# Loading q and k as four tokens of 1 KB on two partition halves, with the last product in two column halves

## The chip, the cores and the metric

The kernel runs on one core of a Trainium2 chip. The metric is the device time of one execution in microseconds, as the median over repeated runs. Before the change the median of 11 runs is 303.47 us (303.08 to 305.29). A core has five engines that run beside each other: PE (TensorE, matrix products; its weight loads are listed apart as PEld), DVE (VectorE), ACT (ScalarE), POOL (GpSimd) and SP (SyncE, which issues most of the transfers here). Sixteen DMA engines move data between HBM and the on-chip memory SBUF, which has 128 partitions. Matrix products land in PSUM.

## What is computed

Attention inside chunks of 64 tokens, and then a bilinear feed-forward layer on its output:

```python
# q, k, v: [8 batches, 8 heads, 576 tokens, 64], float32; chunks of 64 tokens
scores = scale * np.matmul(q_c, k_c.transpose(0, 1, 2, 4, 3))
attn = np.exp(scores - max) / (sum + 1e-09)
x = np.matmul(attn, v_c)          # heads joined: [4608 tokens, 512]
a, b = x @ w_a, x @ w_b           # w_a, w_b: [512, 1536]
out = (a * b) @ w_out             # w_out: [1536, 512], out float32
```

## The kernel before

**Units and blocks.** The 4608 tokens are cut into 18 units of 256 tokens for the attention and into 9 blocks of 512 tokens (two units each) for the feed-forward part. The order of all work on all five engines is written out by hand: each engine runs its instructions in program order and waits where a value isn't there yet.

**Loading a unit.** `load` (line 187) issues the transfers of a unit's q, k and v on SP's queue, and `load_ab` (108) and `load_wo` (137) those of the weights. All of them write into one pool of eight staging tiles named `st`, 4 KB on each of 128 partitions, 512 KB each. A staging tile is free again when a cast (`cast`, 205; `cast_ab`, 117; `cast_wo`, 150) has turned it into 16-bit data. The casts run on POOL, except those of unit 0's q and k, which run on DVE. Since SP issues in order, a load that waits for a free tile holds back all loads behind it. Unit 5's k and all later units are transposed by DMA; q of units 0 to 5 and k of units 0 to 4 (`PE_UNITS`, line 11) are transposed by TensorE, and only those have the layout that the change touches. In this layout a partition holds two neighbouring tokens of all eight heads, so that one contiguous run in HBM is two tokens of one head: 512 bytes. A batch has 576 tokens, so a unit that crosses a batch border comes in two pieces (`pieces`, 168): unit 2 as 64 and 192 tokens, which are 32 and 96 partitions, and unit 4 as 128 and 128 tokens, which are 64 and 64 partitions. Units 0, 1, 3 and 5 are one piece over 128 partitions. v is loaded one token to a partition, in runs of 256 bytes; the panels of w_a and w_b have runs of 1 KB over 128 partitions.

**Transposing.** `transpose_pe` (218) makes eight 128x128 transposes of a tile, and two copies of 512 columns each (line 240) bring the result from PSUM into the tile `qkt`, in the order that `scores` (260) reads. `sums` (290), `inverse` (311) and `values` (318) finish the attention of a unit; the last step of `values` is two multiplies on DVE (line 337), which write the unit's part of `xT`.

**The start.** Lines 663 to 670 put the loads in this order: q and k of unit 0, q and k of unit 1, v of unit 0, panel wb 0, v of unit 1, panel wa 0, then the panels 1 and 2 and (line 682) 3. Then follow q and k of unit 2, panels 4 and 5, v of unit 2, unit 3, w_out, and units 4 and 5 (698 to 718). TensorE runs filler products (`keep_warm`, 97) between the first steps. From line 726 on it runs block 0 through `ab_step` (377), whose products stand at line 389: twelve steps, two for each weight panel, with the transposes of unit 2 behind steps 6 and 7. Block 1 follows with the transposes of units 3 (774, 776), 4 (789) and 5 (793) between its steps. Blocks 2 to 8 run in `Group` (421), with products at line 439.

**The end.** The last block's output is made in two `OutGroup` objects (525), one for each 128-row group `th`, in seven products (line 575) of six matmuls with 256 columns each. The last of them is number 6, first for `th` = 0 and then for `th` = 1. After it DVE scales 256 columns out of PSUM (line 608) and `store` (521) sends 128 rows x 256 columns to HBM, for `th` = 0 on SP's queue and for `th` = 1 on ACT's.

Of the kernel before, what the change touches and what calls it, by code (L numbers as in the profile page):

```python
# [10 lines left out]
PE_UNITS = {"q": 6, "k": 5, "v": 0}  # L11
AB_SCALE = 256.0
OUT_SCALE = 1.0 / AB_SCALE
# [3 lines left out]
def kernel(  # L17
# [10 lines left out]
    nc = tc.nc  # L28
    BF16 = mybir.dt.bfloat16
    FP32 = mybir.dt.float32  # L30
# [7 lines left out]
    B, H, S, D = q.shape  # L38
# [148 lines left out]
    def load(U, names="qkv"):  # L187

        for n in names if U < NU else "":
            src = {"q": q, "k": k, "v": v}[n]  # L190
            if U < PE_UNITS[n]:
                st = st_pool.tile([128, H, 2, D], FP32, name="st")
                for r, b, s, m in pieces(U):
                    nc.sync.dma_start(  # L194
                        out=st[r // 2:(r + m) // 2].rearrange("p h i d -> p h (i d)"),
                        in_=src[b, :, s:s + m, :].rearrange("h (p i) d -> p h (i d)", i=2),
                    )
                staged[n, U] = st.rearrange("p h i d -> p i h d")
            else:
                staged[n, U] = st_pool.tile([128, 2, H, D], FP32, name="st")  # L200
                load_natural(staged[n, U], src, U)
# [3 lines left out]
    def cast(U, names="qkv"):  # L205
        for n in names if U < NU else "":
            if U >= 4 and wo_sums:
                combine_wo(*wo_sums.pop(0))
            raw[n, U] = raw_pool.tile(
                [128, 2, H, D], BF16, name=f"{n}_raw"  # L210
            )
            eng = nc.vector if U == 0 and n != "v" else nc.gpsimd
            eng.tensor_copy(out=raw[n, U], in_=staged.pop((n, U)))


    qkt = {}

    def transpose_pe(U, names="qk"):
        if U not in qkt:
            qkt[U] = qkt_pool.tile([128, 2, 2, NKT, 128], BF16, name="qkt")  # L220
        for n in names:
            w = "qk".index(n)
            src = raw.pop((n, U))
            t = [bank() for _ in range(2 if U < 2 else 1)]
            tp = [
                t[i % len(t)].bitcast(BF16).rearrange("c (i m p) -> c i m p", i=2, m=NKT)[:, i]
                for i in range(2)
            ]
            for i in range(2):
                for m in range(NKT):  # L230
                    nc.tensor.transpose(
                        tp[i][:, m, :],
                        src[:, i, 2 * m:2 * m + 2, :].rearrange("p j d -> p (j d)"),
                        identity,
                    )
            dst = qkt[U][:, w].rearrange("c g m (p i) -> c i m g p", i=2)
            for i in range(2):
                on_dve = i == 0 if U == 0 else w == 0 or U == 1
                cp = nc.vector.tensor_copy if on_dve else nc.scalar.copy
                cp(out=dst[:, i], in_=tp[i].rearrange("c m (g p) -> c m g p", g=2))  # L240

    def transpose_dma(U):
        if U not in qkt:
            qkt[U] = qkt_pool.tile([128, 2, 2, NKT, 128], BF16, name="qkt")
        for w, n in ((0, "q"), (1, "k")):
            if U < PE_UNITS[n]:
                continue
            nc.sync.dma_start_transpose(
                out=qkt[U][:, w].rearrange("p g m c -> p (g m) c"),
                in_=raw.pop((n, U)).rearrange("p g h d -> p (g h d)"),  # L250
            )

# [5 lines left out]
    late = []  # L258

    def scores(U, pools=(None, None), now=2):  # L260
        t = qkt.pop(U)
        E_of[U] = sm_pool.tile([128, 2, NKT, 2, 64], BF16, name="E")
        sc = [bank(p).rearrange("p (m g s) -> p m g s", m=NKT, g=2) for p in pools]
        for m in range(NKT):
            for g in range(2):
                for j in range(2):
                    for cl in range(2):
                        nc.tensor.matmul(
                            sc[j][cl * 64:cl * 64 + 64, m, g, :],
                            t[j * 64:j * 64 + 64, 1, g, m, cl * 64:cl * 64 + 64],  # L270
                            t[j * 64:j * 64 + 64, 0, g, m, cl * 64:cl * 64 + 64],
                            start=m == 0 and g == 0,
                            stop=True,
                            skip_group_check=True,
                        )
        E = E_of[U]
        for j in range(2):
            late.append(
                lambda j=j: nc.scalar.activation(
                    out=E[:, j], in_=sc[j], func=AF.Exp, scale=scale  # L280
                )
            )
        exps(now)
# [34 lines left out]
    def values(U):  # L318
        E, rs, vr = E_of.pop(U), rs_of.pop(U), raw.pop(("v", U))
        K, u = divmod(U, 2)  # L320
        if u == 0:
            x_tiles[K] = x_pool.tile([128, NKT, BLK], FP16, name="xT")
        av = [bank().rearrange("p (m g s) -> p m g s", m=NKT, g=2) for _ in range(2)]
        for m in range(NKT):
            for g in range(2):
                for cl in range(2):
                    for j in range(2):
                        nc.tensor.matmul(  # L328
                            av[cl][j * 64:j * 64 + 64, m, g, :],
                            vr[cl * 64:cl * 64 + 64, g, 2 * m + j, :],  # L330
                            E[cl * 64:cl * 64 + 64, j, m, g, :],
                            start=True,
                            stop=True,
                        )
        for cl in range(2):
            x = x_tiles[K][:, :, 256 * u:256 * u + 256]
            nc.vector.tensor_tensor(
                out=x.rearrange("p m (g c s) -> p m g c s", g=2, c=2)[:, :, :, cl, :],
                in0=av[cl],
                in1=rs[:, cl].rearrange("p m (g s) -> p m g s", g=2),  # L340
                op=MULT,
            )

    def slot(s=None, f=None):

# [175 lines left out]
    def store(K, u, c, o_sb, cols=slice(0, DM), eng=nc.sync):  # L521
        r0 = K * BLK + 256 * u + 128 * c
        eng.dma_start(out=out[r0:r0 + 128, cols], in_=o_sb[:, cols])

    class OutGroup:
# [20 lines left out]
        def part(self, n, th):  # L546
# [24 lines left out]
                lambda: (self.C, a22, t4),  # L571
            )[n]()
            c0 = 0 if one else th * 256
            for kt in range(HFT):
                nc.tensor.matmul(  # L575
                    t[:, c0:c0 + 256],
                    a[:, kt, th * 128:th * 128 + 128],
                    w[:, kt],
                    start=n in (0, 4) and first and kt == 0,
                    stop=last and kt == HFT - 1,  # L580
                    skip_group_check=True,
                )
            if not last:
                return
            if n == 0:
                self.B = self.bank(1)
                nc.scalar.copy(out=self.B, in_=self.A)
            elif n == 1:
                self.o0 = self.tile_of(0)
                nc.scalar.activation(  # L590
                    out=rows(self.o0, lo), in_=halves(self.A), func=AF.Copy, scale=OUT_SCALE
                )
            elif n == 2:
                self.u = self.temp("uo_sb")
                nc.scalar.copy(out=self.u, in_=self.B)
            elif n == 3:
                self.v = self.temp("vo_sb")
                nc.scalar.activation(out=self.v, in_=self.B, func=AF.Copy, scale=OUT_SCALE)
            elif n == 4:
                self.o1 = self.tile_of(1)  # L600
            elif n == 5:
                nc.scalar.activation(
                    out=rows(self.o0, hi), in_=halves(self.B), func=AF.Copy, scale=OUT_SCALE
                )
                for c in [th] if one else range(2):
                    store(self.K, 0, c, self.o0[:, c])
            else:
                nc.vector.tensor_scalar(
                    out=rows(self.o1, lo), in0=halves(self.C), scalar1=OUT_SCALE,
                    scalar2=None, op0=MULT,  # L610
                )
                for c in [th] if one else range(2):
                    store(
                        self.K, 1, c, self.o1[:, c], lo if one else slice(0, DM),
                        nc.scalar if one and th else nc.sync,
                    )
            if n == (3 if one else 4):
                nc.vector.scalar_tensor_tensor(
                    out=rows(self.o1, hi), in0=halves(self.C), scalar=OUT_SCALE,
# [344 lines left out]
```

The softmax here doesn't subtract the row's maximum and nothing guards it: scores larger than these inputs give would overflow.

## Time and profile before

One execution was profiled. It took 304.86 us, and its span from the first to the last instruction is 303.1 us, with a TensorE clock of 1.000.

| What | Value |
|---|---|
| Median of 11 runs | 303.47 us |
| Profiled execution, time and span | 304.86 and 303.1 us |
| PE busy | 292.5 us (97%) |
| PEld busy | 231.9 us (77%) |
| DVE busy | 215.2 us (71%) |
| ACT busy | 196.3 us (65%) |
| POOL busy | 192.6 us (64%) |
| SP's DMA queue | 53.62 MB, 69.7% of 16 engines' span |
| HBM read, written | 37.75 MB, 9.44 MB |
| Whole q tile, issue to landing (median of 4) | 5.7 us |
| Whole k tile, issue to landing (median of 3) | 4.9 us |

How to read it: the busy share of an engine is a mean over stages with different limits, and busy PE time is modelled. The chain of waits that ended last, counted over the whole span, is 82% PE and 7% DMA. In the views by line, `L389` is line 389 of the kernel; in a row, `out<-in` are the written and the read tiles, a number with x is how many instructions the row merges, and brackets hold the idle time of the engine ahead of it and what ended it.

### The profile page before, as it was taken

Reading aid. Unit: us, or ns where it says so; the run is one execution under the profiler, and the core shown is the slowest. Engines: PE = TensorE matmul, PEld = TensorE weight load, DVE = VectorE, ACT = ScalarE, POOL = GpSimd, SP = SyncE. Lnnn points to the kernel's source line nnn. Section 1 sums busy time; section 2 is a strip of 40 time slices with the busy share of each in tenths; the row PEclk is TensorE's granted clock in tenths of the full one; section 3 lists DMA queues with packets and bytes.
Section 4 is the critical chain, followed back from the end, with each engine's and each line's share of the span. In section 5 each row is a group of like instructions: output and inputs, shape, how many; then the busy total and the mean of one; then the engine's idle time right before and its main releaser. Section 6 shows DMA issues by size and latency. Waiting matters only on the chain.

```text
span 303.1 us, 8590 instructions
## 1 busy us (share of the span) xinstructions
PE 292.5 (97%) x3521; PEld 231.9 (77%) x3521; DVE 215.2 (71%) x341; ACT 196.3 (65%) x355; POOL 192.6 (64%) x180
## 2 busy tenths in 40 slices
PE   6799899999999999999999999999999999999995
PEld 2344467866588888888888888888888888888884
DVE  3457675777789597669676967696769667965773
ACT  2743557448387768676867696768676877567532
POOL 0665658995999688908890889088808801790560
PEclk9999999999999999999999999999999999999999
DMA  7999999999999999895949494949541001100015
GB/s 228 313 367 267 286 326 352 228 221 225 225 247 252 225 212 277 184 230 160 227 107 228 147 220 113 240 141 208 118 89 75 2 2 69 71 1 3 2 76 201
DMA packets 140983, 54.29 MB, mean 179 GB/s; under 512 B 117136, under 2 KB 135056, under 8 KB 140944
## 3 DMA queue, kind: packets, MB, share of 16 engines
q1 hardware_dynamic: 140800, 53.62, 69.7%
q8 instruction: 27, 0.44, 0.6%
q10 hardware_dynamic: 144, 0.13, 0.1%
q14 instruction: 12, 0.10, 0.1%
HBM read 37.75 MB, written 9.44 MB: 156 GB/s over the span
## 4 chain that ended last, share of the span: by engine, by line
PE 82%; DMA 7%; DVE 3%; SPq 3%; ACT 1%; POOL 1%; issue 1%; DVEq 0%; ACTq 0%
PE pb L439 18%; PE pc L439 12%; PE pa L439 12%; PE po L575 12%; PE pq L575 10%; DMA st<-in_moe_w_b_dram 3%; PE pb L643 3%; DMA st<-in_moe_w_a_dram 2%; PE po L389 2%; PE pc L389 2%; PE pa L389 2%; PE pq L389 2%; DMA st<-in_v_dram 2%; PE pt L295 2%; PE pt L328 2%; SPq L194 1%
## 5 line engine op out<-in xcount | busy, mean ns | idle before, releaser
L519 POOL TENSOR_TENSOR so<-ab_sb 128x512 f16<-128x512 f16 x23 | 27.4, 1191 | 70.1 <-DVE ab_sb L489 70.1
L439 PEld LDWEIGHTS <-t 128*128 128x128 f16 x504 | 48.3, 98 | 8.8 <-issue 2.3
L439 PE MATMUL pb<-s,wa 128*128 128x256 f16 x336 | 50.6, 273 | 0.0
L439 PE MATMUL pa<-xT,wb 128*128 128x256 f16 x336 | 50.4, 273 | 0.0
L477 DVE TENSOR_TENSOR c_sb<-pc,v_sb 128x512 f32<-128x512 f32 x42 | 28.9, 687 | 25.5 <-ACT v_sb L450 25.5
L575 PEld LDWEIGHTS <-ab_sb 128*128 128x128 f16 x384 | 37.6, 98 | 4.7 <-issue 0.4
L439 PEld LDWEIGHTS <-wb 128*128 128x128 f16 x336 | 32.9, 98 | 4.0
L439 PEld LDWEIGHTS <-wa 128*128 128x128 f16 x336 | 31.8, 98 | 4.2 <-issue 0.2
L489 DVE SCALAR_TENSOR_TENSOR ab_sb<-pc,c_sb 128x512 f16<-128x512 f32 x42 | 29.0, 689 | 7.8 <-PE pc L439 6.3
L450 ACT COPY u_sb<-pb 128x512 f32<-128x512 f32 x42 | 24.7, 588 | 14.9 <-PE pb L439 14.7
L489 DVE SCALAR_TENSOR_TENSOR ab_sb<-pb,b_sb 128x512 f16<-128x512 f32 x42 | 29.0, 690 | 6.2 <-PE pb L439 5.2
L457 ACT COPY pb<-pa 128x512 f32<-128x512 f32 x42 | 24.1, 573 | 10.7 <-PE pa L439 10.3
L575 PEld LDWEIGHTS <-so 128*128 128x128 f16 x288 | 28.1, 98 | 3.4
L450 ACT COPY b_sb<-pa 128x512 f32<-128x512 f32 x42 | 25.0, 595 | 7.2 <-PE pa L439 7.1
L478 DVE TENSOR_TENSOR pc<-pc,u_sb 128x512 f32<-128x512 f32 x42 | 28.9, 688 | 0.0
L519 POOL TENSOR_TENSOR so<-so,ab_sb 128x512 f16<-128x512 f16 x23 | 27.1, 1178 | 1.7
L450 ACT COPY v_sb<-pb 128x512 f32<-128x512 f32 x42 | 24.7, 587 | 5.1 <-PE pb L439 4.4
L519 POOL TENSOR_TENSOR ab_sb<-ab_sb 128x512 f16<-128x512 f16 x23 | 26.9, 1169 | 0.0
L519 POOL TENSOR_TENSOR so<-ab_sb,so 128x512 f16<-128x512 f16 x23 | 26.1, 1160 | 0.0
L439 PE MATMUL pc<-s,t 128*128 128x256 f16 x168 | 25.2, 273 | 0.2 <-DVE ab_sb L489 0.2
L439 PE MATMUL pb<-s,t 128*128 128x256 f16 x168 | 25.3, 273 | 0.0
L439 PE MATMUL pc<-xT,t 128*128 128x256 f16 x168 | 25.2, 272 | 0.1
(129 smaller groups left out, 572.4 us busy)
## 6 DMA issues: line engine op xcount, KB each, us to landing
out_dram<-o_sb SPq DMA_DIRECT2D x34, 256.0 KB, 2.3
st<-in_v_dram SPq DMA_DIRECT2D x32, 256.0 KB, 4.6
st<-in_k_dram SPq DMA_DIRECT2D x25, 256.0 KB, 4.5
st<-in_q_dram SPq DMA_DIRECT2D x23, 256.0 KB, 3.7
st<-in_moe_w_b_dram SPq DMA_DIRECT2D x6, 512.0 KB, 7.3
st<-in_moe_w_a_dram SPq DMA_DIRECT2D x6, 512.0 KB, 7.3
st<-in_moe_w_out_dram SPq DMA_DIRECT2D x6, 512.0 KB, 6.5
st<-in_q_dram SPq DMA_DIRECT2D x4, 512.0 KB, 5.7
```

Source lines behind the costliest of these rows:

```text
L295: nc.tensor.matmul(sm[cl][j * 64:j * 64 + 64, :], ones[cl * 64:cl * 64 + 64, :], E[cl * 64:cl * 64 + 64, j].rearrange("p m g s -> p (m g s)"),
L328: nc.tensor.matmul(av[cl][j * 64:j * 64 + 64, m, g, :], vr[cl * 64:cl * 64 + 64, g, 2 * m + j, :], E[cl * 64:cl * 64 + 64, j, m, g, :], st ...
L389: nc.tensor.matmul(ps[n], w_ab[n, i][:, kt, o:o + 128], xT[:, kt, c0:c1], start=(kt == 0), stop=(kt == NKT - 1),)
L439: nc.tensor.matmul(t[:, h * 256:h * 256 + 256], w[:, kt, h * 128:h * 128 + 128], x[:, kt], start=start and h == 0 and kt == 0, stop=h == 1 ...
L450: nc.scalar.copy(out=t, in_=src)
L457: nc.scalar.copy(out=self.B, in_=self.A)
L477: nc.vector.tensor_tensor(out=self.c, in0=self.C, in1=self.v, op=ADD)
L478: nc.vector.tensor_tensor(out=self.C, in0=self.C, in1=self.u, op=ADD)
L489: nc.vector.scalar_tensor_tensor(out=self.dst[:, :, c0:c0 + 256], in0=t.rearrange("p (h n) -> p h n", h=2), scalar=AB_SCALE, in1=o.rearran ...
L519: (eng or nc.gpsimd).tensor_tensor(out=o, in0=x0, in1=x1, op=op)
L575: nc.tensor.matmul(t[:, c0:c0 + 256], a[:, kt, th * 128:th * 128 + 128], w[:, kt], start=n in (0, 4) and first and kt == 0, stop=last and ...
L643: nc.tensor.matmul(out_ps[K, tg], ab_tiles[K][:, ft, tg * 128:tg * 128 + 128], wo_sb[:, ft], start=(ft == 0), stop=(ft == NFT - 1),)
```

## The change

It has three parts.

1. **Loads of q and k of the units transposed by TensorE.** A partition now holds four neighbouring tokens of four heads. Heads 0 to 3 go to partitions 0 to 63 and heads 4 to 7 to partitions 64 to 127, with one transfer for each half of the partitions. A contiguous run is four tokens of one head: 1 KB. Each piece of a unit is so two transfers: a whole unit is two of 64 partitions, unit 2 is two of 16 and two of 48, unit 4 is four of 32. The casts write the same number of elements under another view. The eight transposes of a tile take the four tokens in turn, two head pairs each. The two copies into `qkt` write every fourth element instead of every second, and `qkt` of these tiles is in the order head pair, token; `qkt_view` gives `scores` and `transpose_dma` the same indices for both orders.
2. **Unit 1's last multiply** (line 337, second chunk half) is two multiplies of 256 columns instead of one of 512.
3. **The last product of the kernel** (number 6, `th` = 1) is made in two halves of 128 columns: six matmuls of 128 columns, a scaling of 128 columns and a store of 128 rows x 128 columns on SP's queue, and then the same for the other columns with the store on ACT's queue.

```diff
             if U < PE_UNITS[n]:
-                st = st_pool.tile([128, H, 2, D], FP32, name="st")
+                st = st_pool.tile([128, 4, 4, D], FP32, name="st")
                 for r, b, s, m in pieces(U):
-                    nc.sync.dma_start(
-                        out=st[r // 2:(r + m) // 2].rearrange("p h i d -> p h (i d)"),
-                        in_=src[b, :, s:s + m, :].rearrange("h (p i) d -> p h (i d)", i=2),
-                    )
+                    for o in range(2):
+                        nc.sync.dma_start(
+                            out=st[64 * o + r // 4:64 * o + (r + m) // 4].rearrange(
+                                "p h i d -> p h (i d)"
+                            ),
+                            in_=src[b, 4 * o:4 * o + 4, s:s + m, :].rearrange(
+                                "h (p i) d -> p h (i d)", i=4
+                            ),
+                        )
...
-            eng.tensor_copy(out=raw[n, U], in_=staged.pop((n, U)))
+            dst = raw[n, U]
+            if U < PE_UNITS[n]:
+                dst = dst.rearrange("p a (b h) d -> p (a b) h d", b=2)
+                raw[n, U] = dst
+            eng.tensor_copy(out=dst, in_=staged.pop((n, U)))
...
+    def qkt_view(U, n):
+
+        t = qkt[U][:, "qk".index(n)]
+        if U < PE_UNITS[n]:
+            return t.rearrange("c (m g p) -> c g m p", m=NKT, g=2)
+        return t.rearrange("c (g m p) -> c g m p", g=2, m=NKT)
...
-            for i in range(2):
-                for m in range(NKT):
+            for i in range(4):
+                for m in range(2):
+                    o = (i % 2) * 256 + m * 128
                     nc.tensor.transpose(
-                        tp[i][:, m, :],
+                        tp[i // 2][:, o:o + 128],
                         src[:, i, 2 * m:2 * m + 2, :].rearrange("p j d -> p (j d)"),
                         identity,
                     )
-            dst = qkt[U][:, w].rearrange("c g m (p i) -> c i m g p", i=2)
+            dst = qkt_tile(U)[:, w].rearrange("c (o m q i) -> c i m o q", o=2, m=2, i=4)
...
-            nc.vector.tensor_tensor(
-                out=x.rearrange("p m (g c s) -> p m g c s", g=2, c=2)[:, :, :, cl, :],
...
+            for m in (slice(0, 2), slice(2, 4)) if (U, cl) == (1, 1) else [slice(0, 4)]:
+                nc.vector.tensor_tensor(
+                    out=x.rearrange("p m (g c s) -> p m g c s", g=2, c=2)[:, m, :, cl, :],
...
+            end = n == 6 and one and th == 1
+            for cols in (slice(0, 128), slice(128, 256)) if end else [slice(0, 256)]:
+                for kt in range(HFT):
+                    nc.tensor.matmul(
+                        t[:, c0:c0 + 256][:, cols],
...
+                if end:
+                    nc.vector.tensor_scalar(
+                        out=rows(self.o1, cols), in0=self.C[:, cols], scalar1=OUT_SCALE,
+                        scalar2=None, op0=MULT,
+                    )
+                    store(
+                        self.K, 1, th, self.o1[:, th], cols, nc.scalar if cols.start else nc.sync
+                    )
```

## The prediction

> **What bounds the kernel now.** I read the page's slices first, then the chain of waits, then the DMA rate stage by stage.
>
> The slices:
>
> ```profile
> PE   6799899999999999999999999999999999999995
> ...
> DMA  7999999999999999895949494949541001100015
> ```
>
> Each digit is a fortieth of the span, 7.6 us. After the start TensorE is full to the end: what is lost in the first 45 us is lost for good, and what is won can only be won there or in the last 3 us. DMA is full over the first sixteen slices, so the question is which of the two releases the other early on. The chain of waits, in order of time (start, length, what):
>
> ```profile
> 9.70 4.99 DMA st<-in_v_dram
> ...
> 14.73 1.05 POOL v_raw L213
> ...
> 16.16 9.23 DMA st<-in_moe_w_b_dram
> ...
> 25.44 1.05 POOL wb L120
> ...
> 27.36 6.34 DMA st<-in_moe_w_a_dram
> ...
> 33.76 1.05 POOL wa L120
> ...
> 34.85 1.04 PE pc L389 x4
> ```
>
> Up to 34.85 us the program is DMA arrivals with casts between them. TensorE's own rows agree: it waits for unit 2's q (0.80 us) and then for the fifth wa panel:
>
> ```profile
> 4.69 0.69 DVE L213 CAST q_raw<-st 128x1024 bf16<-128x1024 f32 x1 [3.49 <-DMA st<-in_q_dram]
> ...
> 9.26 1.04 POOL L213 CAST k_raw<-st 128x1024 bf16<-128x1024 f32 x1 [0.51 <-DMA st<-in_k_dram]
> ...
> 30.83 0.62 PE L231 MATMUL pt<-identity,q_raw 128*128 128x128 bf16 x8 [0.80 <-POOL q_raw L213]
> ...
> 34.85 1.04 PE L389 MATMUL pc<-xT,wa 128*128 128x512 f16 x4 [0.28 <-POOL wa L120]
> ```
>
> The first four tiles (q0, k0, q1, k1, 524 KB each) are cast at 4.69, 6.18, 7.71 and 9.26, so they land 1.51 us apart. Now the rate by stage (length, busy time of five engines, clock, DMA share, GB/s last):
>
> ```profile
> 3.00:4.50 1.50, 1.50 (x5) 0.40 (x3) 0.00 (x0) 0.00 (x0) 0.00 (x0) 1.00 1.15 347
> 20.00:21.50 1.50, 1.50 (x9) 0.68 (x8) 0.48 (x1) 0.59 (x1) 1.02 (x1) 1.00 1.09 386
> 24.50:26.00 1.50, 1.50 (x9) 0.68 (x8) 1.05 (x3) 0.36 (x2) 0.56 (x1) 1.00 1.27 231
> 26.00:27.50 1.50, 1.50 (x9) 0.68 (x8) 1.50 (x3) 0.36 (x2) 0.48 (x1) 1.00 1.17 226
> 39.00:40.50 1.50, 1.50 (x38) 0.69 (x36) 1.05 (x1) 1.47 (x3) 0.83 (x2) 1.00 1.13 341
> 53.00:54.50 1.50, 1.50 (x15) 1.34 (x16) 1.13 (x4) 0.88 (x4) 1.50 (x2) 1.00 1.23 251
> ```
>
> Lines one and five are q/k tiles in one DMA over 128 partitions with 512 B runs: 347 and 341 GB/s. Line two is weights in 1 KB runs, 128 partitions: 386. Lines three and four are unit 2's q and k, the same 512 B runs, but cut by the batch border into 32 and 96 partitions: 231 and 226. Line six is unit 4, cut into 64 and 64 partitions. Its finer slices from 51.5 to 54.5 us, where the first few still hold the wide w_out rows, sit near 212:
>
> ```profile
> GB/s 369 328 335 280 335 239 212 212 198 246 253 218 212 198 239 184 212 225 232 219 205 205 253 253 266 280 287 478 219 294 198 198 225 198 184 198 212 280 307 287
> ```
>
> Same packets, same queue, engines full: what differs is the number of partitions in one DMA.
>
> [...]
>
> **The change, part by part.**
>
> *Loads of q (units 0 to 5) and k (0 to 4).* 15 issues become 30, packets halve in number and double to 1 KB, and every DMA now covers partitions 0 to 63 or 64 to 127, or a part of those. The nearest row is unit 4: I take 225 GB/s, bounds 212 and 250. A tile then takes 0.524/0.225 = 2.33 us instead of 1.51, 0.82 more. The first is cheaper: by 3.0 us about 138 KB have moved anyway (48, 88 and 140 GB/s in three half microseconds), and the other 386 KB take 1.72 instead of 1.11, 0.61 more. So k1 lands 0.61 + 3 x 0.82 = **3.07 us later** (2.2 at 250, 3.5 at 212). v0, wb0, v1 and wa0 queue behind in the same order, and so does unit 1's whole ACT and DVE train, which hangs on k_raw at 9.26. Nothing hides it: DMA was never idle there.
>
> *Unit 2.* Before: 1.05 MB at 228 is 4.6 us by rate, though the casts of wa3 (27.86) and k2 (31.25) lie only 3.4 apart, so landings do not follow the mean rate wholly. After: each tile is two DMAs of 16 partitions and two of 48. [...] I take **1.0**, since the landings lagged less than the rate said; bounds 0 and 2.4.
>
> *Unit 3.* Whole tiles again, each 0.82 later. q's cast ends at 41.49, needed by TensorE at 42.10: slack 0.61. k's ends at 43.00, needed at 43.88: slack 0.88 against 1.64. TensorE waits 1.64 - 0.88 = **0.76** more (0 to 1.3). *Units 4 and 5*: [...] unit 5's q loses 0.82. Cast ends and use lie 3.2 us apart (k of unit 4: 60.14 to 63.32) and 3.7 (q of unit 5: 64.88 to 68.59): hidden, at most 0.8 if POOL, busy without a gap there, has moved too.
>
> *SP.* An unhindered issue is 0.45 us, so eight take 4 us while their data take over 9: hidden behind the transfers. Behind the first eight stand v0, wb0, v1, wa0; later ones stand in front of w_out loads that wait for buffers anyway. 0.
>
> *Casts, transposes, copies.* As many elements and instructions; copies of L240 write every fourth element instead of every second, 0.72 us each now for 512 elements, no dearer per element than the 0.69 of full-width DVE rows. 0; if the wider step did cost, two copies on the path before scores(1) bound it by 0.7. A gain is excluded, the count being the same.
>
> *Unit 1's last multiply in halves.* 512 columns cost 0.69 and 256 cost 0.42, so the first half is ready 0.27 earlier and TensorE could start at 17.52 instead of 17.79. It then meets the weight waits at 28.95 and 34.85, set by DMA: 0. Were DMA not the bound, 0.27 would be won.
>
> *The last product.* 12 matmuls of 128 columns for 6 of 256: transposes show 8 such in 0.45 us, 0.056 each, so 0.67 against 0.66. The last DVE row falls from 0.42 to about 0.29 by the same slope. The stores: 128 KB land in 1.7 us and 256 KB in 2.3, so 64 KB would land in 1.4, but the first half's issue stands behind the other row group's at 299.80 (0.38) on SP and runs beside the last. I take **-0.2**; bounds -0.45 and 0.
>
> Sum: 3.07 + 1.0 + 0.76 - 0.2 = **+4.6 us**: a span of 307.7 from 303.1. The profiled execution took 304.86, 1.4 above the median of the runs; the same 4.6 on the median 303.47 gives **308.1**.
>
> **Rivals.**
> *Longer packets win (the other side).* If 64 partitions cost nothing, a tile takes 0.524/0.386 = 1.36 us instead of 1.51: 4 x 0.15 = 0.6 won by k1, 0.2 at the tail, perhaps 0.3 in unit 2: 302.4. It decides as soon as a half-partition DMA runs above 347 GB/s, that is if k_raw of unit 1 starts before 9.26. For it: 386 against 347 in the rows above. Against: line six and the slices, where 64-partition pieces in the same order run at 212 to 251. 0.08.
> *Half hidden.* [...] units 2 and 3 cost nothing: 3.07 shrinks to about 1.3, less 0.2: 304.6. For it: 251 in line six is above 212, and landings beat the rate in unit 2. [...] 0.10.
> *More is lost.* TensorE's fillers no longer bridge waits that grow by 0.8 us each, and it slows[...]. The trace's long gaps are near 1 us and its clock row stays full. With unit 2 at its upper bound (1.4 more), POOL late in unit 4 (0.8) and a clock halved for 2 us (1.0): 4.6 + 3.2, 311.3. 0.12.
>
> **How the numbers follow.** The forecast has 0.70. Its own range, from the bounds of the loads, is 305.9 to 310; with most of the half-hidden case and part of the dear one, 304.4 to 311.0 holds 8 in 10. A difference under 0.2% (0.6 us) can't be told from none here. Faster is the first rival with a little of the tail's gain, 0.09; the same 0.04, the thin end of the half-hidden case; slower 0.87.
>
> **What would show it.** Right: DMA near 225 GB/s from 3 to 11 us with packets of 1 KB; casts of q0, k0, q1, k1 about 2.3 us apart and the last near 12.3; first L389 matmul near 20.6; the wait for wa near 38.9; TensorE waiting for unit 3's k near 48; a last DVE row near 0.29. Wrong: a rate over 300 GB/s there, or k1 before 10; a first L389 late by 3 us but the end late by less than 1; a stall after 60 us on q or k of units 4 and 5.

## The result: 2.85% slower, and the profile after

The changed kernel takes 312.61 us (median; 311.59 to 313.3), the kernel before in the same comparison 303.73. The ratio is 1.0285, with a 95% interval of 1.0268 to 1.0302: **8.9 us slower**, where 4.6 were forecast. The profiled execution has a span of 309.8 us against 303.1. The two traces so show 6.7 of the 8.9 us, since the profiled execution before was 1.4 us above its median and the changed one 1.0 below.

The page's slices of the changed kernel, 7.7 us each:

```profile
PE   6789988998999999999999999999999999999995
...
DMA  7999999899999999697749685879342101200025
```

TensorE has new losses in its first ten slices, up to 77 us, and none later. DMA is as full in the first sixteen as it was, but for one slice. The rates by stage of the changed kernel (length, busy time of five engines, clock, DMA share, GB/s):

```profile
3.00:4.50 1.50, 1.50 (x5) 0.39 (x3) 0.00 (x0) 0.00 (x0) 0.00 (x0) 1.00 1.04 267
4.50:6.00 1.50, 0.35 (x1) 0.00 (x0) 0.41 (x1) 0.00 (x0) 0.00 (x0) 1.00 1.05 249
6.00:7.50 1.50, 1.16 (x9) 0.88 (x9) 0.29 (x1) 0.08 (x1) 0.00 (x0) 1.00 1.12 244
```

The engines are nearly as full as before (1.04 to 1.12 against 1.15), at 244 to 267 GB/s where 347 were moved. The casts of the first tiles, in the timelines of DVE and POOL:

```profile
7.76 0.69 DVE L222 CAST k_raw<-st 128x1024 bf16<-128x1024 f32 x1 [1.47 <-DMA st<-in_k_dram]
```

```profile
9.92 1.04 POOL L222 CAST q_raw<-st 128x1024 bf16<-128x1024 f32 x1 [8.62 <-DMA st<-in_q_dram]
12.21 1.04 POOL L222 CAST k_raw<-st 128x1024 bf16<-128x1024 f32 x1 [1.25 <-DMA st<-in_k_dram]
```

k1 is cast at 12.21 instead of 9.26, 2.95 us later; 3.07 were forecast. The missing time is elsewhere. The chain of waits up to 45 us (start, length, what) now runs over one transfer only, k of unit 0, and then over copies and TensorE:

```profile
2.83 4.84 DMA st<-in_k_dram
7.76 0.70 DVE k_raw L222
...
9.58 1.33 ACT qkt L261
...
12.18 4.74 DVE qkt L261 x4
...
39.05 1.41 ACT qkt L261
```

`qkt` at L261 are the copies out of PSUM, L240 before. Their durations, before and then after (minimum, median, maximum in ns, first and last start):

```profile
L240 DVE COPY qkt<-pt x10: 710/722/745, 6.8 to 69.9; 128x512 bf16<-128x512 bf16 x10
L240 ACT COPY qkt<-pb x5: 729/737/741, 6.1 to 64.6; 128x512 bf16<-128x512 bf16 x5
```

```profile
L261 DVE COPY qkt<-pt x10: 1287/1318/1350, 8.4 to 77.0; 128x512 bf16<-128x512 bf16 x10
L261 ACT COPY qkt<-pb x5: 1299/1323/1407, 7.4 to 70.8; 128x512 bf16<-128x512 bf16 x5
```

The same 512 elements take 1.32 us instead of 0.72 to 0.74, on both engines. Unit 1's four copies run on DVE while ACT copies nothing, and take the same 1.29 to 1.34 us, so it isn't two engines that write one tile at once.

TensorE is slower too. Its first rows for unit 0, before and then after, and the six fillers behind scores(1) after:

```profile
5.45 0.40 PE L231 MATMUL pt<-identity,q_raw 128*128 128x128 bf16 x4 [0.59 <-DVE q_raw L213]
5.68 0.39 PE L231 MATMUL pb<-identity,q_raw 128*128 128x128 bf16 x4
```

```profile
6.34 0.61 PE L252 MATMUL pt<-identity,q_raw 128*128 128x128 bf16 x4 [1.49 <-DVE q_raw L222]
6.75 0.63 PE L252 MATMUL pb<-identity,q_raw 128*128 128x128 bf16 x4
...
19.34 2.18 PE L101 MATMUL pc<-warm_in 128*128 128x512 bf16 x6
```

From the start of one row to the next, four transposes take 0.41 us instead of 0.23; the six fillers take 2.18 instead of 1.47. The clock column shows 1.00 all the while, so this has to be read from durations. It begins before the first copy and goes with the loads: in the seven traces with the loads of before (among them e1_old_loads, below) TensorE first reaches its full rate by about 6.5 us; in the four with all loads of the change and no fillers added (the changed kernel, e2_step2, e3_gather, e5_two_queues) between about 17 and 23. What it costs in the changed kernel was not measured apart.

### The profile page after: what moved, and what is told of

It reads as the page before. It is cut to its first block, busy times and chain, and to the rows that moved or that the text cites. A ratio compares the mean times of both kernels' runs of the same rounds, so it can differ in the third digit from the quotient of the medians.

```text
span 309.8 us, 8634 instructions
## 1 busy us (share of the span) xinstructions
PE 296.4 (96%) x3527; PEld 234.2 (76%) x3527; DVE 219.5 (71%) x343; ACT 200.8 (65%) x355; POOL 193.5 (62%) x180
## 4 chain that ended last, share of the span: by engine, by line
PE 87%; DVE 5%; ACT 3%; issue 2%; DMA 2%; SPq 1%; DVEq 0%; ACTq 0%
PE pb L464 18%; PE pc L464 12%; PE pa L464 12%; PE po L602 12%; PE pq L602 9%; PE po L414 3%; PE pb L414 3%; PE pb L675 3%; DVE qkt L261 2%; PE pc L414 2%; PE pt L352 2%; PE pt L319 2%; DMA st<-in_k_dram 2%; ACT qkt L261 1%; PE pa L414 1%
## 5 line engine op out<-in xcount | busy, mean ns | idle before, releaser
L362 DVE TENSOR_TENSOR xT<-pt,ln 128x512 f16<-128x512 f32 x29 | 18.8, 686 | 9.4 <-PE pt L352 5.8
```

What stands on the lines that cost most here:

```text
L362: nc.vector.tensor_tensor(out=x.rearrange("p m (g c s) -> p m g c s", g=2, c=2)[:, m, :, cl, :], in0=av[cl][:, m], in1=rs[:, cl, m].rearra ...
```

## The experiments

Each median is compared with runs of the kernel before on the same chip (303.7 to 304.1 us). Because the profiled execution before was above its median, spans of other runs stand about 1 us better against its 303.1 than their times do. In e1_old_loads, e2_step2, e12_fillers and e14_copies_alone the columns of `qkt` stand in another order than `scores` takes them, so the values of the output are others; the work is the same. The "ports theory" of some expectations is the author's name for the guess that transfers to half of the partitions make the loss; no run here shows a port.

| Run | us | ratio to before, 95% |
|---|---|---|
| e1_old_loads | 309.85 | 1.0197 [1.0175, 1.0218] |
| e14_copies_alone | 310.67 | 1.0220 [1.0200, 1.0241] |
| e2_step2 | 307.63 | 1.0122 [1.0095, 1.0149] |
| e3_gather | 308.07 | 1.0133 [1.0107, 1.0158] |
| e12_fillers | 310.27 | 1.0210 [1.0175, 1.0245] |
| e6_halves_512 | 307.75 | 1.0129 [1.0092, 1.0165] |
| e9_head_halves | 305.65 | 1.0054 [1.0036, 1.0072] |
| e10_middle | 308.85 | 1.0147 [1.0108, 1.0186] |
| e13_even_odd | 305.76 | 1.0066 [1.0043, 1.0089] |
| e5_two_queues | 312.51 | 1.0287 [1.0244, 1.0331] |
| e8_two_queues_gather | 305.92 | 1.0071 [1.0040, 1.0102] |
| e4_parts23 | 304.27 | 1.0014 [1.0000, 1.0027] |
| e7_tail_order | 303.97 | 1.0009 [0.9994, 1.0024] |
| e11_gather_before | 303.58 | 0.9987 [0.9969, 1.0004] |
| e15_gather_alone | 303.34 | 0.9987 [0.9971, 1.0004] |

### Which part costs what

**The old loads under everything else of the change.**

```diff
-                    for o in range(2):
-                        nc.sync.dma_start(out=st[64 * o + r // 4:...], in_=src[b, 4 * o:4 * o + 4, ...])
+                    nc.sync.dma_start(
+                        out=st[r // 2:(r + m) // 2].rearrange("p a (b i) d -> p (a b) (i d)", i=2),
+                        in_=src[b, :, s:s + m, :].rearrange("h (p i) d -> p h (i d)", i=2),
+                    )
```

> Loads of q and k as before (one DMA over 128 partitions, 512 B runs, units 2 and 4 cut at the batch border as before); all else as in the changed kernel, the copies into qkt included, so heads and tokens stand in another order and the scores pair other tokens. Ports theory (half-partition DMAs make the loss): no loss is left, 303.3 to 304.3 us, copies of L261 still 1.3 us but hidden. Copies theory (the copies' writes to every fourth element cost 0.6 us more each, and stand on the path from k of unit 1 to the first L389 product and later in ACT's and DVE's order): 308 to 310 us, with the first four casts back at 4.7, 6.2, 7.7 and 9.3 us.

6.0 of the 8.9 us remain with the loads of before. So most of the loss can't be the loads.

**Copies with half the step.** The loads of the change, copies with as many dimensions and as many elements, but writing every second element (4 bytes apart) instead of every fourth (8 bytes).

```diff
-            dst = qkt_tile(U)[:, w].rearrange("c (o m q i) -> c i m o q", o=2, m=2, i=4)
+            dst = qkt_tile(U)[:, w].rearrange("c (j m o q i) -> c j i m o q", j=2, m=2, o=2, i=2)
...
-                    out=dst[:, 2 * i:2 * i + 2],
+                    out=dst[:, i],
```

> Loads as in the changed kernel; only the copies into qkt write every second element instead of every fourth, with the same four dimensions, so tokens stand in another order in qkt. Copies theory with the step as its cause: a copy takes 0.72 us again and the time falls to 305 to 307 us. If the fourth dimension is the cause: 1.3 us a copy and 312 to 313 us. Ports theory: 311 us or more even with a copy of 0.72 us, since k of unit 1 still lands near 12 us.

312.61 falls to 307.63, a little over the 305 to 307 that were expected, and the copies are back at their old price:

```profile
L261 DVE COPY qkt<-pt x10: 711/723/743, 8.7 to 72.9; 128x512 bf16<-128x512 bf16 x10
L261 ACT COPY qkt<-pb x5: 728/737/745, 7.6 to 67.6; 128x512 bf16<-128x512 bf16 x5
```

With as many dimensions, a step of 4 bytes takes 0.72 and 0.74 us and one of 8 bytes 1.32: here the step of the write made the difference, not the number of dimensions.

**The order of the change, written in runs.** The transposes put the four tokens of one head pair side by side in one PSUM bank. The copies then read with a step and write contiguously; `scores` finds what it expects.

```diff
-            for i in range(4):
-                for m in range(2):
-                    o = (i % 2) * 256 + m * 128
+            for m in range(2):
+                for i in range(4):
...
-                        tp[i // 2][:, o:o + 128],
+                        tp[m][:, i * 128:i * 128 + 128],
...
-                    in_=tp[i].rearrange("c (i m o q) -> c i m o q", i=2, m=2, o=2),
+                    in_=tp[i].rearrange("c (i o q) -> c o q i", i=4, o=2),
```

> Loads as in the changed kernel; the transposes put the four tokens of one head pair side by side in one bank, and each copy reads every 128th element of PSUM and writes runs of 256 elements in order. Copies theory, if only the write side counts: 0.72 us or less a copy, 305 to 307 us. If a step on the read side costs as much as one on the write side: 1.3 us or more, 312 us or more. Ports theory: 311 us or more either way.

```profile
L260 DVE COPY qkt<-pt x10: 681/681/692, 8.7 to 73.4; 128x512 bf16<-128x512 bf16 x10
L260 ACT COPY qkt<-pb x5: 585/585/592, 7.3 to 68.0; 128x512 bf16<-128x512 bf16 x5
```

Cheaper than before the change, above all on ACT, and yet 308.07 us, no less than with copies of 0.72 and over the 305 to 307 expected. The first product of block 0 comes at 21.24, 0.7 us before that of e2_step2, and TensorE then waits 1.0 us for a `wa` panel: with the copies cheap, transfers set the time. The read with a step from PSUM didn't make these copies dearer (0.681 us on DVE and 0.585 on ACT, against 0.723 and 0.737).

**The step alone, on the kernel before.**

```diff
-            dst = qkt[U][:, w].rearrange("c g m (p i) -> c i m g p", i=2)
+            dst = qkt[U][:, w].rearrange("c g m p -> c (g m p)").rearrange(
+                "c (o m q i) -> c i m o q", o=2, m=2, i=4
+            )
```

> The kernel before, whose copies out of PSUM write every fourth element of qkt as in the change; so the columns of qkt stand in another order and the output is not the reference's. Nothing else differs. If the copies are the term that was missing: 1.32 us a copy instead of 0.72 to 0.74, and +5.5 us, 309.0 to 310.0. If the gain from the old loads was an interplay with the changed end and the split multiply, and the copies count for the two on the path before scores(1) only: at most +1.2 us, under 305.3.

**6.8 us** from one access pattern. Where they go, in the chain of waits of this run from 5 to 20 us:

```profile
6.13 0.69 DVE k_raw L213
6.82 2.36 DVE qkt L242 x2
...
10.13 4.73 DVE qkt L242 x4
```

All four copies of unit 1 run on DVE in one row. They took from 9.24 to 12.14 before and take from 10.13 to 14.86 now; TensorE's waits up to 52 us say the same (engine, tile, line, what it waited for: total us, times, longest):

```profile
PE po L275 <- DVE qkt L242: 3.2, 1, 3.2
PE pb L275 <- DVE qkt L242: 1.4, 1, 1.4
PE pa L275 <- ACT qkt L242: 0.8, 1, 0.8
```

A wait of 3.2 us has a second price. These are the six fillers behind scores(1), before and in this run, and then this run by stage (PE busy, clock, DMA share, GB/s):

```profile
14.16 1.47 PE L101 MATMUL pc<-warm_in 128*128 128x512 bf16 x6
```

```profile
17.29 2.74 PE L101 MATMUL pc<-warm_in 128*128 128x512 bf16 x6
```

```profile
13.00:15.00 2.00, 0.10 (x8) 0.85 1.14 322
15.00:17.00 2.00, 2.00 (x69) 0.50 1.09 376
17.00:19.00 2.00, 2.00 (x9) 0.50 1.08 373
```

At half clock (0.50) scores(1), 2.7 us late (14.90 against 12.19), becomes a first product of block 0 that is 4.3 late (22.05 against 17.79). Here the clock fell to 0.50 behind one wait of 3.2 us; in e6_halves_512, below, it fell behind two shorter ones, 1.33 and 1.64 us with 0.8 us of work between them: it is 0.72 from 7.5 to 9 us and 0.50 in the row after it.

**Parts two and three alone** (the split multiply and the last product in halves, as in the diff of the change, on the kernel before).

> The kernel before with unit 1's last multiply in halves and the last product in column halves, loads and copies untouched. Both theories: 0.1 to 0.4 us under the kernel before, all of it at the end; the split multiply starts the first L389 product about 0.27 us earlier and this is eaten by the waits for weights by 35 us. If the split multiply counts, up to 0.7 us.

0.4 to 0.5 us slower, at the edge of what can be told; 0.1 to 0.4 us faster was expected.

### The loads

**Half the partitions, with the old runs.** The kernel before, whole q and k tiles in two transfers of 64 partitions, runs of 512 bytes.

```diff
+                    step = m // 2 if m == UNIT else m
+                    for c in range(0, m, step):
...
-                        out=st[r // 2:(r + m) // 2].rearrange("p h i d -> p h (i d)"),
+                            out=st[(r + c) // 2:(r + c + step) // 2].rearrange("p h i d -> p h (i d)"),
```

> The kernel before with one edit: q and k of the units that are one piece (0, 1, 3 and 5) are loaded by two transfers of 64 partitions each, in the old layout with 512 B runs. Ports theory: the casts of q0, k0, q1, k1 move from 4.7, 6.2, 7.7, 9.3 to about 5.6, 7.8, 9.9, 12.2 us, as in the changed kernel, and the time rises by 2.5 to 4 us to 306.3 to 307.8. Rival (the four-head split or the 1 KB runs make the loads slow): casts as before and no loss, 303.5 to 304.3 us.

**Two transfers of all 128 partitions**, cut by heads 0 to 3 and 4 to 7 instead.

```diff
+                    for h in (slice(0, 4), slice(4, 8)) if m == UNIT else [slice(0, H)]:
...
-                        out=st[r // 2:(r + m) // 2].rearrange("p h i d -> p h (i d)"),
+                            out=st[r // 2:(r + m) // 2, h].rearrange("p h i d -> p h (i d)"),
```

> The kernel before with q and k of units 0, 1, 3 and 5 loaded by two transfers each, as in e6, but cut by heads: each transfer has 256 KB in 512 B runs and covers all 128 partitions. Ports theory: partitions decide, not number or size, so the casts of q0, k0, q1, k1 stay at 4.7, 6.2, 7.7, 9.3 us (within 0.4) and the time at 303.4 to 304.4 us. Rival (twice as many transfers of half the size cost it): as e6, casts near 5.5, 7.9, 10, 12.2 us and 307 to 308 us.

**64 partitions, but the even ones and then the odd ones.** Number, size and runs as in e6_halves_512.

```diff
+                    step = 2 if m == UNIT else 1
+                    for c in range(step):
...
-                        out=st[r // 2:(r + m) // 2].rearrange("p h i d -> p h (i d)"),
+                            out=st[r // 2:(r + m) // 2][c::step].rearrange("p h i d -> p h (i d)"),
```

> The kernel before, with q and k of units 0, 1, 3 and 5 loaded in two transfers each, the even partitions and then the odd ones. Number of transfers, partitions in each (64), runs (512 bytes) and bytes are those of the cut in contiguous halves; only which partitions they are differs. If the place of the partitions limits the rate [...]: 300 to 345 GB/s between 6 and 10.5 us, casts of units 0 and 1 at 4.4, 6.8, 8.4 and 9.9 as in the cut by heads, and 305 to 306 us. If the number of partitions in one transfer limits it, wherever they lie, it is as slow as the contiguous halves: 230 to 260 GB/s, unit 1's k cast at 12.0 to 12.3 and 307 to 308.5 us.

The three runs' rates from 6 us on, contiguous halves, heads, even and odd:

```profile
6.00:7.50 1.50, 0.84 (x9) 0.51 (x9) 0.12 (x1) 0.66 (x1) 0.00 (x0) 1.00 1.21 261
7.50:9.00 1.50, 0.34 (x4) 0.35 (x5) 1.09 (x2) 0.07 (x1) 0.00 (x0) 0.72 1.24 243
```

```profile
6.00:7.50 1.50, 0.13 (x1) 0.00 (x0) 0.66 (x2) 0.68 (x1) 0.00 (x0) 1.00 1.14 342
7.50:9.00 1.50, 1.05 (x10) 0.56 (x10) 1.29 (x3) 0.73 (x1) 0.62 (x1) 1.00 1.16 338
```

```profile
4.50:6.00 1.50, 0.71 (x5) 0.37 (x5) 0.69 (x1) 0.00 (x0) 0.00 (x0) 1.00 0.82 237
...
7.50:9.00 1.50, 0.74 (x8) 0.74 (x9) 1.43 (x3) 0.00 (x0) 0.00 (x0) 1.00 1.10 323
9.00:10.50 1.50, 1.50 (x33) 0.63 (x35) 0.64 (x1) 0.73 (x1) 1.04 (x1) 1.00 1.19 314
```

With contiguous halves the engines are fullest (1.21 to 1.24) and move least. Casts of q1 and k1 come at 10.03 and 12.22 there, 2.19 apart; at 9.06 and 10.62 with even and odd partitions, 1.56 apart, as in the kernel before (1.55). So it isn't the number of partitions in a transfer that slows it, but **which** ones, and e6_halves_512 takes about 2 us more than e13_even_odd (4.0 against 1.9 over the kernel before). Why the place counts isn't shown.

A second, smaller cost showed up in both fast cuts, which still lose 1.5 and 1.9 us (at most 0.6 was expected of the cut by heads). With even and odd partitions, in the row at 4.50, the DMA share is 0.82 and the rate 237. q0 to k0 take 2.62 us (4.89 to 7.51) instead of 1.49, and after that the tiles come at full pace. The engines are short of work there (0.82, against 1.10 and 1.19 from 7.5 us on); whether the doubled number of transfers makes it was not tried apart.

**A middle and two outer pieces**, partitions 32 to 95 and then 0 to 31 and 96 to 127:

```diff
+                    for c, n1 in ((64, 128), (0, 64), (192, 64)) if m == UNIT else [(0, m)]:
```

> As e6, but a tile is cut into partitions 32 to 95 (one transfer of 64), 0 to 31 and 96 to 127 (two of 32). [...] Ports theory: 0.76 us for the middle piece at 347 GB/s and 0.6 us for each outer one at about 218 to 250, 1.8 to 1.96 us a tile, so k1 is cast at 10.4 to 11.1 us, before that of e6 although there are more transfers, and slices of 340 GB/s stand between slices of 220. Rival (64 partitions are slow whichever they are): k1 at 12 us or later, no slice over 290 GB/s.

Undecided, and a miss for what was expected of k1. Casts at 6.56, 8.49, 10.37 and 12.26: 1.9 us apart, between the two cases (1.56 and 2.19), but the same gap at the start (143 GB/s from 3.75 to 4.50) is larger here and eats it.

**The second halves on ACT's queue**, so that both halves are under way together, in the changed kernel:

```diff
-                        nc.sync.dma_start(
+                        (nc.scalar if o and U < 2 else nc.sync).dma_start(
```

> The changed kernel, but the second half (partitions 64 to 127) of q and k of units 0 and 1 is issued on ACT's queue, so that both halves are in flight together; sizes, runs and number of transfers are the same. Ports theory: [...] the rate from 3 to 8 us rises from about 245 GB/s to 340 to 385, k of unit 1 is cast near 9 us instead of 12.2, and the time falls by 2 to 3.5 us to 309 to 310.5. Rival (short or many transfers are slow in themselves, or SP's issues are the limit only by their number): the rate stays under 280 GB/s and the time at 312 to 313 us.

```profile
4.50:6.00 1.50, 0.35 (x1) 0.00 (x0) 0.50 (x1) 0.00 (x0) 0.00 (x0) 1.00 1.10 247
6.00:7.50 1.50, 1.25 (x9) 0.87 (x9) 0.19 (x1) 0.18 (x1) 0.00 (x0) 1.00 1.13 245
```

No gain in time. In these rows the rate is that of the changed kernel (247 and 245 GB/s here, 249 and 244 there). SP's queue is far ahead of ACT's from 4.5 to 5.5 us, and the two are even from 8.75 to 9.75 (q1 is SP's and q10 ACT's: packets, MB, share of 16 engines):

```profile
q1 hardware_dynamic: 186, 0.18, 81.3%
q10 hardware_dynamic: 68, 0.07, 30.2%
```

```profile
q10 hardware_dynamic: 174, 0.17, 54.4%
q1 hardware_dynamic: 181, 0.16, 53.9%
```

In the second stretch both halves are under way together, 0.33 MB in 1 us (330 GB/s) where the changed kernel moves 247, and k of unit 1 is cast 1.48 us behind q (10.04 and 11.52) instead of 2.29. So two halves at once were faster here (e8_two_queues_gather, which stands next, moves 335 GB/s from 9 to 10.5 us, where the changed kernel moves 255); why SP's queue was ahead before isn't shown. The time doesn't gain from it, as DVE's dear copies of unit 1 end no earlier: scores(1) starts at 16.87 against 16.95.

**The best of the change's layout:** two queues and contiguous writes for units 0 and 1, the loads of before for the others, the split multiply, the old end.

```diff
+            if U < 2 and U < PE_UNITS[n]:
...
+                        (nc.scalar if o else nc.sync).dma_start(
```

> The four-token loads for units 0 and 1 alone, their halves on SP's and ACT's queues, with copies that gather from PSUM and write runs of 256 elements; unit 1's last multiply in halves; all later units and the end as in the kernel before. If both findings hold [...], nothing of the loss is left and the 1 KB runs pay: the casts of q0, k0, q1, k1 end up to 0.6 us earlier than before, and the time is 302.7 to 303.8 us. If not: 305 us or more.

305.92, still 2.2 us over the kernel before: with cheap copies, too, these loads of two units keep a loss.

### TensorE early, and the end

**More fillers in e2_step2**, 21 more at the start, so that TensorE isn't slow in its waits.

```diff
-        keep_warm(8)
+        keep_warm(14)
...
-        transpose_pe(1)
+        transpose_pe(1, "q")
+        keep_warm(6)
+        transpose_pe(1, "k")
...
```

> e2_step2 (the changed kernel's loads, copies with a step of two) with more filler products on TensorE while it waits in the first 16 us: 14 for 8, 5 for 1, 5 for 2, 6 new between unit 1's q and k, 3 for 1. If the lower rate of TensorE there (128-column transposes at 0.10 us instead of 0.056) is a part of the loss: scores and fillers of unit 1 run at full rate, the first L389 product comes 0.7 to 1 us earlier than in e2, and the time is 0.4 to 1 us under e2's. If not, or if later waits eat it: the time of e2, 307.3 to 308 us.

The first product of block 0 came at 20.55 instead of 21.94, earlier as expected, and yet the kernel is 2.6 us slower (2.3 if each is set against its own runs of the kernel before), where 0.4 to 1 us faster was expected. TensorE's waits from 15 to 52 us, with fillers and then without:

```profile
PE pb L252 <- POOL k_raw L222: 1.7, 1, 1.7
PE pb L414 <- POOL wb L120: 0.4, 1, 0.4
...
PE pc L414 <- POOL wa L120: 0.3, 1, 0.3
```

```profile
PE pb L252 <- POOL k_raw L222: 0.3, 1, 0.3
PE pa L414 <- DVE xT L362: 0.2, 1, 0.2
```

The 1.4 us won went into three waits for transfers, 2.4 us in all, the longest for unit 3's k, which the prediction had named. So early lateness hides transfers behind it here, and the time won by removing it is not paid out. Why the rest was lost stays open; unit 3's k was cast 1.1 us later (47.1 against 46.0) as well.

**The end in another order**: other row group between the two halves.

```diff
-            for th in range(2):
+            for th in (1, 0):
...
+        ends[1].part(6, 1, slice(0, 128))
+        ends[0].part(6, 0)
+        ends[1].part(6, 1, slice(128, 256))
```

> The kernel before with the last product in column halves, but the other row group's product stands between the halves, and that group goes second in all products after the first two. If the wait of the second half's first matmul for the scaling of the first half (0.38 us in the changed kernel's trace) makes the loss at the end: the wait is gone, a last scaling of 0.29 us, and 0.1 to 0.5 us under the kernel before. If the extra store or the extra scaling makes it: 0.2 to 0.5 us over.

The changed kernel's timeline shows what this order avoids, first PE and then DVE:

```profile
305.62 0.50 PE L602 MATMUL pa<-wot,ab_sb 128*128 128x128 f16 x6
306.50 0.49 PE L602 MATMUL pa<-wot,ab_sb 128*128 128x128 f16 x6 [0.38 <-DVE o_sb L611]
```

```profile
306.16 0.28 DVE L611 TENSOR_SCALAR o_sb<-pa 128x128 f32<-128x128 f32 x1
307.03 0.29 DVE L611 TENSOR_SCALAR o_sb<-pa 128x128 f32<-128x128 f32 x1 [0.59 <-PE pa L602]
```

The second half's products wait for the scaling of the first half, though they write other columns of `pa`; the trace shows this wait, not the reason for it. From the start of the last `po` product to ACT's issue it is 2.40 us (304.96 to 307.36) against 1.97 before (298.49 to 300.46). In the new order the wait is gone and the last scaling starts at 299.42 instead of 300.00; the time, 303.97, is the same as before within its interval, so the 0.1 to 0.5 us that were expected were not seen.

**Contiguous writes for the kernel before**, with the split multiply and that end, and alone:

```diff
-            for i in range(2):
-                for m in range(NKT):
+            for m in range(NKT):
+                for i in range(2):
...
-            dst = qkt[U][:, w].rearrange("c g m (p i) -> c i m g p", i=2)
+            dst = qkt[U][:, w].rearrange("c g (j m) (p i) -> c j m g p i", j=2, i=2)
...
+                    in_=tp[i].rearrange("c (m i) (g p) -> c m g p i", m=2, g=2),
```

> The kernel before with its own loads, and three edits that the runs so far point to: the copies into qkt read PSUM with a step and write runs in order, unit 1's last multiply is in halves, and the last product's halves stand on either side of the other group's product. Copies take 0.58 to 0.69 us instead of 0.72 to 0.74 if the gather pays with pairs as it did with fours. Expected 0.2 to 0.6 us under the kernel before; if a gather of pairs is dearer than one of fours, copies of 0.7 us or more and no difference.

> The kernel before, with the transposes of one head pair side by side in one PSUM bank, so that its copies read with a step and write contiguous runs; loads, end and multiply as before. If a copy that writes contiguously is worth something on the path: copies of 0.59 and 0.68 us instead of 0.74 and 0.72, 0.2 to 0.6 us under the kernel before. If the early stage waits for transfers anyway: within 0.2 us of it.

Both 0.9987 with intervals that just hold 1. The copies are 0.587 us on ACT (0.737 before) and 0.682 on DVE (0.722), and scores(1) starts at 11.51 instead of 12.19, but TensorE then waits 0.3 us for a `wb` panel: the early stage still hangs on transfers. No version was shown to beat the kernel before.

## Why the prediction was wrong

The direction was right, and half-partition loads were slow as forecast; the size was missed by 4.3 us, and one term did that.

- **Casts, transposes, copies: the step that failed.** It read "0; if the wider step did cost, two copies on the path before scores(1) bound it by 0.7". Alone the wider step costs 6.8 us (e14_copies_alone); in the changed kernel taking it away gives back 5.0 (312.61 to 307.63). Three things were wrong in it. The price: a count of elements was taken for a price, and "no dearer per element" was argued from rows with other patterns; it is 1.32 us for 0.72. The count: unit 1's four copies all run on DVE, one behind another, so 4 x 0.6 = 2.4 us stand before scores(1), not two copies. And what follows: in e14_copies_alone TensorE at half clock after the gap (0.50 from 15 us on, behind 3.2 us), and in the changed kernel in units 2 to 5 again copies on the path (0.8 us waits for ACT at 40.50 and 72.27; two ACT copies of 2.45 us at 49.31 hold back the copy of L422 for which TensorE waits 0.43 at 52.03). The first product of block 0 came at 23.09, where 20.6 was forecast, and the start of scores falls back by 4.7 us in unit 2, 5.8 in unit 3, 6.7 in unit 4 and 7.2 in unit 5.
- **Loads of units 0 and 1: 3.07, measured 2.95 for k1** and right in kind, but so near by luck: q0 came 0.90 us later where 0.61 was forecast, and the next three tiles 2.05 later where 2.46 was, as the rate was 244 to 267 GB/s and not 225. "What differs is the number of partitions in one DMA" was a wrong reading (e13_even_odd). In the changed kernel, though, k1 isn't what is waited for: DVE's four copies run without a gap from 12.18 to 16.90, and k1 lands under them. What of the loads is on the path is k0, 1.58 later (7.76 against 6.18), with TensorE's lower rate behind it. That is why the parts don't add: 6.8 for the copies, 4.0 for whole tiles in halves and 0.5 for the rest are 11.3, and together they cost 8.9.
- **Unit 2: 1.0, measured about 0.** The 1.0 was the author's estimate, with a rate for 16 partitions that no trace backed. The unit's k is cast at 32.03 against 31.25, but by then TensorE needs it later too, and no wait is left. With cheap copies (e2_step2) all loads and the end cost 3.8, of which 0.4 to 0.5 are the end; the 4.8 forecast for the loads was about 1.4 too much.
- **Unit 3: 0.76.** Not in the changed kernel, where TensorE comes too late to wait. Unit 3's k is waited for in e6_halves_512 (0.4 us) and in e12_fillers (1.7). The loads of units 4 and 5 were hidden, as forecast; what TensorE waits for there (0.81 and 0.45 us, at 72.27 and 78.50) are copies.
- **The split multiply: 0, right.** In e4_parts23 steps ahead were up to 0.3 us earlier and the end wasn't.
- **The last product: -0.2, measured +0.46 with the split multiply.** The term counted two short products beside the first half's scaling; instead they wait for it (0.38). The last scaling did fall to 0.29. A store of 64 KB instead of 128 didn't shorten what follows ACT's issue by more than 0.2 us (2.44 against 2.60); it landed 1.6 us after its issue, where 1.4 was forecast.
- **SP: 0.** Not the limit in the changed kernel: with half of the issues on ACT's queue (e5_two_queues) k0 is cast at 7.67 against 7.76. The gap at the start of e9_head_halves (247 and 231 GB/s from 3.75 to 5.25 us) was not foreseen.
- **The rivals.** "Longer packets win" asked for over 347 GB/s and is out at 244 to 267; runs of 512 bytes in the same halves (e6_halves_512) move 232 to 261, so the longer run gives little there. "More is lost", 311.3, comes nearest in number, and its slow TensorE came, with these loads. But the copies aren't in it, and its largest term, 1.4 more for unit 2, didn't come. Its halved clock was the author's estimate: the clock fell to 0.50 in e14_copies_alone, but not in the changed kernel. Against the rival stood that the clock row stays full; that row stays full in the changed kernel too, where TensorE is slow.

## What to carry to other kernels

A change of layout in HBM is paid where the layout is undone: before pricing the transfers, write down the byte step of every write behind them, and if no row of the trace has that step, allow for what it did here (1.32 us for 0.72) and multiply by all copies in a row on that engine. Where an order must be undone between PSUM and SBUF, read with the step and write in runs (0.68 and 0.585 us here). If a load must be cut, cut it by its free dimension and not into contiguous partition halves: here 1.5 us lost against 4.0, and none uncut.

## What was not expected of the hardware

- Copies of 512 bf16 elements to each partition, PSUM to SBUF: a write step of 8 bytes took 1.32 us on DVE and on ACT (the changed kernel); 4 bytes 0.72 and 0.74 (the kernel before, e2_step2); contiguous 0.68 and 0.585 (e3_gather). Twice the step took almost twice the time; why isn't shown.
- Even and odd partitions loaded at 314 to 323 GB/s from 7.5 to 10.5 us (e13_even_odd, DMA share 1.10 to 1.19), contiguous halves at 243 to 261 from 6 to 10.5 us (e6_halves_512), with the engines fuller (1.21 to 1.24).
- Two queues to two halves moved 0.18 and 0.07 MB from 4.5 to 5.5 us, and 0.16 and 0.17 MB, side by side at 330 GB/s, from 8.75 to 9.75 (e5_two_queues).
- TensorE ran at little more than half its rate (four transposes in 0.41 us instead of 0.23) up to about 17 to 23 us in the traces with the loads of the change, under a clock column of 1.00.
